# Where attention's masked sums are written, and where its row statistics are taken

## The chip, the cores and the metric

The kernel runs on one core of a Trainium2 chip. A core has a matrix engine (TensorE, PE in the profile, with its weight loads as PEld), VectorE (DVE), ScalarE (ACT), GpSimd (POOL) and SyncE (SP), whose queue issues most DMA transfers here. Each engine works through its own instructions in order and waits on semaphores for the others. The metric is device time in microseconds (us), the median over runs; lower is better.

## The reference, cut to what matters

Four layers act on `x` (2048 rows, width 512, fp32): a linear-attention layer A, a segmented attention layer B, and the same two again. Each normalizes its input's rows and adds its output to `x`.

```python
def _layernorm(x, axis=-1, eps=1e-5):
    m = jnp.mean(x, axis=axis, keepdims=True)
    v = jnp.var(x, axis=axis, keepdims=True)
    return (x - m) / jnp.sqrt(v + eps)
...
# layer B: 32 heads of width 16, 4 segments of 512 rows
for s in range(N):
    logits = jnp.einsum("bhqd,bhkd->bhqk", qs, ks) * scale + mask
    p = _softmax(logits, axis=-1)
    a_dot = jnp.einsum("bhqk,bhkd->bhqd", p, vs)
    ...
    a_mem = num / den
    o = g * a_mem + (1.0 - g) * a_dot
...
x = x + _A_ref(_layernorm(x, axis=-1), A_wqkv, A_w_phi, A_wo)
x = x + _B_ref(_layernorm(x, axis=-1), B_wq, B_wk, B_wv, B_wo, B_beta)
x = x + _A_ref(...)
x = x + _B_ref(...)
```

Two things bear on the change: every row of layer B's input needs its mean and variance, and every softmax row needs the maximum of its masked logits.

## The kernel before, in words

**Layer A** (`LayerA`) has two passes. `pass1` normalizes the rows, projects them and sums the key features. `pass2` goes through 16 tiles of 128 rows: it multiplies query features with the sums, divides (`weigh`, line 494), transposes and splits the result into a high and a low part (`turn`, line 465, tiles `oh` and `ol`), and multiplies by the output weights in `out_proj` (line 484). The end of `out_proj` is the function `end` (line 488): VectorE adds the product in PSUM to the rows of `x` (in a tile `xr` or `ot`, loaded by `residual`), and SP stores the sum to DRAM as layer B's input.

**Layer B** (`LayerB`) works in 4 segments of 512 rows. Per segment it normalizes the rows, projects queries, keys and values, and attends in 8 half-chunks `m` of 4 heads, so 32 half-chunks a layer and 64 in the kernel. Its `norm` (line 958) runs `norm_T` (line 426): load four tiles of rows into `x`; per tile `moments` (line 379: `bn_stats` and `bn_aggr` on VectorE, into a small tile `st`); `guard` adds the epsilon; `root` and `refine` make the inverse root; ACT normalizes each tile; `columns` transposes it. Each yield of this generator is placed by hand (`n`, `ln`, `load` in the tables).

For a half-chunk, `stack` lays the operands out by DMA (`e<-ta`); `maxima` (line 1150) finds each softmax row's maximum; `put_maxima` (line 1183) transposes the maxima, negates them on ACT into a tile `mt`, and stores them by a DMA of the ACT queue as one more row of the query operand, so that the exponential in `attend` (line 1192) needs no further subtraction. `maxima` has five passes. In each, PE writes logits into two PSUM banks, `mx` and `my`, of which there is one buffer each; then `top` (line 1163) runs on VectorE once per piece: add the mask, take the maximum, and write the masked sums back over the logits. The instruction that hands out the maximum appears in the profile as a second one, `DVE_READ_ACCUMULATOR2_ANT` on `mxs`. Three of the five passes hold two pieces per bank (widths 128 and 384, or twice 256), two hold a single piece of 512. The masked sums themselves are never read. PE's next pass needs the banks, and so waits for the last readout of each.

The memory part of layer B divides by denominators. `close` and `read` call `invert` (line 1038), which puts its steps on a calendar: `compact` loads 16 x 512 or 8 x 512 denominators into a tile `dn` (`dn<-den` on SP), `flip` takes the reciprocal on VectorE, `put` stores it (`inv<-dn` on SP), `spread` and `load` bring it back in the layout needed. In a layer's last segment, chunks 2 and 3 call it from `read`, so that its `compact` falls on the step of another chunk's `put`.

**What sets the order.** All engines are wrapped (`Ordered`, line 153), so each engine's instructions stay in the order in which the Python program issues them. In layer B that order comes from hand-written tables (`FIRST`, `GAPS`, `LAST`, `FINAL`, lines 52 to 101) with five steps per half-chunk: each step names the projections, norm steps and maxima to issue beside attention's own work. The end of layer A's pass 2 is issued inside the first steps of layer B (`steps`, line 1346, argument `side`; slots -9 to 1), and the beginning of layer B, with the norm of its first segment, inside pass 2 (`opening`, line 1331). Semaphore waits are worked out from the tiles: an instruction that writes a tile region waits for earlier readers and writers of it, on its own engine too, and a tile with `bufs=1` waits for the last use of its predecessor.

Of the kernel before, what the change touches and what calls it, by code (L numbers as in the profile page):

```python
# [18 lines left out]
P = 128  # L19
NSEG = 4  # L20
NC = D // P
NT = T // P
# [5 lines left out]
OT = 3  # L28
TA = 8
OO = 5  # L30
MT = 2
PV = 1
G = 3
R = 5
# [73 lines left out]
def interleave_kernel(ctx, tc, x_in, a_wqkv, a_wphi, a_wo, b_wq, b_wk, b_wv, b_wo, b_beta,  # L108
# [19 lines left out]
    def T2(tag, bufs, dt=F32, shape=(P, 512)):  # L128
        return sp.tile(list(shape), dt, tag=tag, bufs=bufs, name=nm(tag))
# [10 lines left out]
    def wait(f):  # L140

        if put_off[0] is None:
            f()
        else:
            put_off[0].append(f)
# [54 lines left out]
    share = cp.tile([P, 8], F32, name="share")  # L200
    gated = cp.tile([P, NC, 4], F32, name="gated")
    ones = cp.tile([32, P], F32, name="ones")

    def constants():

# [173 lines left out]
    def moments(st, t, x):  # L379
        bs = T2("bs", 2, shape=(P, 6))  # L380
        dve.bn_stats(bs, x)
        dve.bn_aggr(st[:, t, 0:2], bs)
# [40 lines left out]
            return wtiles(spare)  # L423
        return [hp_.tile([P, NC, D], F32R, tag=tag, bufs=1, name=nm(tag)) for tag in ("hh", "hl")]

    def norm_T(xsrc, s, hT, spare=None, slow=False, off=False):

        st = T2("st", 2, shape=(P, 4, 8))
        xt = rows_of(xsrc, s)
        yield  # L430
        for t, x in enumerate(xt):
            moments(st, t, x)
            if t < 3:
                yield
        guard(st)
        yield
        root(st)
        if slow:
            yield
        refine(st, pool if off else dve)  # L440
        if slow:
            yield
        for t in range(4):
            normal(st, t, xt[t])
            if slow and t < 3:
                yield
        yield
        hT[:] = htiles(spare)
        for t in range(4):
            columns(hT, t, xt[t])  # L450
            yield
# [32 lines left out]
    def out_proj(x, xdst, i, o, w):  # L484
        po = PS("g", G)
        yield from mm3(po, lambda a, kc: o[a][:, kc * P : (kc + 1) * P], lambda b, kc: w[b][:, kc, :])

        def end():
            dve.tensor_tensor(out=x, in0=po, in1=x, op=ADD)
            sync.dma_start(out=xdst[i], in_=x)  # L490
        wait(end)
        yield

# [106 lines left out]
    class LayerA:  # L600
# [4 lines left out]
        def first(self, hT, vv, upcoming):  # L605

            xt = rows_of(self.xsrc, SEGS[0])
            wph = T2("U", 2)[:, 0 : NC * DH].rearrange("p (c f) -> p c f", c=NC)
            sync.dma_start(out=ident, in_=c_ident)
            sync.dma_start(out=bd, in_=c_bd)  # L610
            sync.dma_start(out=wph, in_=a_wphi.rearrange("(c h) d f -> (h d) c f", c=NC))
            kraw, vraw, qraw = [fetch(a_wqkv[:, i * D : (i + 1) * D]) for i in (1, 2, 0)]
            st = T2("st", 2, shape=(P, 4, 8))
            hT[:] = htiles()
            (vh, vl), (kh, kl), (qh, ql) = wv, wk, wq = [wtiles(tag) for tag in ("w8", "w8", "e8")]
            for key, w in (("awv", wv), ("awk", wk), ("awq", wq)):
                kept[key] = [dtile((P, NC, D), nm(key)) for _ in range(2)]
                owed.extend(zip(kept[key], w))

            def low(eng, w, kc, raw):  # L620
                eng.tensor_tensor(out=w[1][:, kc, :], in0=raw, in1=w[0][:, kc, :].bitcast(F32), op=SUB)

            for t in range(4):
                moments(st, t, xt[t])
            guard(st)
            root(st)
            refine(st, dve)
            for c in range(NC):
                pool.tensor_tensor(out=phibd[:, c], in0=wph[:, c, :].unsqueeze(1).broadcast_to([P, 8, DH]),
                                        in1=bd[:, 16:24].unsqueeze(2).broadcast_to([P, 8, DH]), op=MUL)  # L630
            kf, qf = [], []
            kfold, qfold = folded(kraw, kf), folded(qraw, qf)
            normal(st, 0, xt[0])
            for t in (1, 3):
                dve.tensor_scalar(xt[t], xt[t], st[:, t, 2:3], st[:, t, 3:4], op0=MUL, op1=ADD)
            next(kfold)
            next(kfold)
            normal(st, 2, xt[2])
            columns(hT, 0, xt[0])
            columns(hT, 1, xt[1])  # L640
            next(kfold)
            next(kfold)
            columns(hT, 2, xt[2])
            columns(hT, 3, xt[3])
            next(kfold)
            upc = upcoming(1)
            next(upc[1])
            for kc in range(NC):
                act.copy(vh[:, kc, :], vraw[kc])
                low(pool if kc % 2 else dve, wv, kc, vraw[kc])  # L650
            for kc in range(NC):
                act.copy(kh[:, kc, :], kf[kc])
                low(dve, wk, kc, kf[kc])
            vt = v_tile(hT, wv, vv, ("g", G))
            for t in range(4):
                for _ in range(4):
                    next(vt)
                if t == 1:
                    for _ in range(4):
                        next(qfold)  # L660
                for _ in range(NEXT[t]):
                    next(upc[1])
            next(qfold)
            for kc in range(NC):
                act.copy(qh[:, kc, :], qf[kc])
                low(dve, wq, kc, qf[kc])
            return wq, wk, wv, upc
# [271 lines left out]
    class LayerB:  # L939
# [17 lines left out]

        def norm(self, s):
            self.hT[s] = []
            return norm_T(self.xsrc, s, self.hT[s], slow=True, off=True)  # L960

        def values(self, s):

# [74 lines left out]
        def invert(self, s, c, k, parts):  # L1038


            lo, hi = 8 * parts[0], 8 * parts[-1] + 8
            n = (hi - lo) * 4
            tiles = {}

            def compact():
                d = tiles["d"] = T2("dn", 2, shape=(P, 64))
                sync.dma_start(out=d[:, 0:n], in_=self.den(s, c)[lo:hi].rearrange("h (x i) -> (h x) i", i=n))

            def flip():
                dve.reciprocal(tiles["d"][:, 0:n], tiles["d"][:, 0:n])  # L1050

            def put():
                tiles["i"] = dtile((hi - lo, D), nm("inv"))
                sync.dma_start(out=tiles["i"].rearrange("h (x i) -> (h x) i", i=n), in_=tiles["d"][:, 0:n])

            def spread():
                wide = tiles["w"] = dtile((hi - lo, DH, D), nm("wide"))
                sync.dma_start(out=wide, in_=tiles["i"].unsqueeze(1).broadcast_to([hi - lo, DH, D]))

            def load():  # L1060
                for i in parts:
                    t = self.inv[s, c, i] = T2(*(("mmq", 2) if i else ("KN", 1)))
                    sync.dma_start(out=t, in_=tiles["w"][8 * i - lo : 8 * i - lo + 8].rearrange("h d n -> (h d) n"))
            for j, f in zip((0, 1, 2, 3, 5) if s < NSEG - 1 else (0, 2, 3, 4, 6), (compact, flip, put, spread, load)):
                self.at(k + j, f)
# [84 lines left out]
        def maxima(self, m):  # L1150


            s, c, hf = m // 8, m % 8 // 2, m % 2
            Q, K = [t[:, 2 * hf : 2 * hf + 2, :] for t in self.st[s, c]["set"]]
            mx = T2("mxs", 2, shape=(P, 16))

            def prod(pb, r, i, at, w):
                for e in range(2):
                    q, k = Q[64 * e : 64 * e + 63, r, :], K[64 * e : 64 * e + 63, r, :]
                    mm(pb[e][:, at : at + w], lhsT=q[:, i * P : (i + 1) * P], rhs=k[:, 0:w],  # L1160
                       start=True, stop=True, tile_position=(64 * e, 0))

            def top(pb, e, r, i, at):
                n = (i + 1) * P
                col = (e * 2 + r) * 4 + i
                pl = pb[e][:, at : at + n]
                with tc.high_priority():
                    dve.tensor_tensor_reduce(
                        out=pl, in0=pl, in1=mask[:, 512 - n : 512], scale=1.0, scalar=-3.0e38,
                        op0=ADD, op1=MAX, accum_out=mx[:, col : col + 1])  # L1170

            for what in ([(0, 0, 0), (0, 2, P)], [(0, 3, 0)], [(1, 0, 0), (1, 2, P)],
                         [(0, 1, 0), (1, 1, 256)], [(1, 3, 0)]):
                pb = [PS(t, 1) for t in ("mx", "my")]
                for r, i, at in what:
                    prod(pb, r, i, at, max(256, (i + 1) * P))
                for e in range(2):
                    for r, i, at in what:
                        top(pb, e, r, i, at)
                self.mx[m] = mx  # L1180
                yield

# [359 lines left out]
```

## Time and profile before

| | |
|---|---|
| median of 3 runs | 1481.35 us (1480.6 to 1843.29) |
| the profiled execution's own time | 1477.25 us |
| its span | 1475.5 us |
| granted TensorE clock, mean | 0.985 |
| stage: layer A 1, pass 1 | about 0 to 180 us |
| stage: pass 2, then its overlap with attention | about 180 to 270, and to 310 us |
| stage: attention 1 (layer B) | about 270 to 735 us |
| stage: layer A 2 | about 735 to 985 us, pass 1 to about 900 |
| stage: attention 2 | about 985 to 1475 us |

How to read it: the profile gives busy time of each engine and the idle time before its instructions with the engine and tile that ended it, in square brackets or behind `<-`. In a row such as `x512 | 254.8, 498 | 181.7 <-PE`, the numbers are the count, busy time in us, the mean of one in ns, and idle time before them. `mx<-mx,mask` means that tile `mx` is written from `mx` and `mask`. All operations recorded by a helper share that helper's line: L163 is the wrapper, L185 and L189 are the matmul helpers, so the tiles tell the operations apart. A VectorE row named `CUSTOM_DVE_ANT_0` is a `top`; `BATCH_NORM_STATS2` and `BATCH_NORM_AGGREGATE` are `moments`.

### The profile page before, as it was taken

The numbers are of one execution on the slowest core, as the hardware profiler recorded it, in microseconds if no ns is written. First come the engines' busy times: TensorE is split into PE (matmuls) and PEld (weight loads), VectorE is DVE, ScalarE is ACT, GpSimd is POOL, SyncE is SP. The second block draws the span as 40 slices with busy tenths as digits, with TensorE's granted clock in tenths as the row PEclk, the third lists the DMA queues.
The fourth block names the chain that finished last, engine by engine and source line by source line (L and its number), as shares of the span: only waits on it lengthen the run. The fifth ranks groups of instructions, "written<-read, shape, count | busy, mean of one in ns | idle before, by whom it ended". The sixth has DMA issues, their size and how long they took to land.

```text
span 1475.5 us, 32962 instructions
## 1 busy us (share of the span) xinstructions
PE 1395.7 (95%) x12052; PEld 960.0 (65%) x12052; DVE 1022.0 (69%) x3007; ACT 810.8 (55%) x1228; POOL 731.6 (50%) x1066
## 2 busy tenths in 40 slices
PE   7989999999999999998899999999999999999987
PEld 6778778765566566655567887886555565566544
DVE  4766877777667767677446677867776776766762
ACT  5546345446576576565534434543656766755652
POOL 1668754224455556454424456631345556645532
PEclk9999999999999999999999999999999999999998
DMA  5387375546556556567630105764565574565451
GB/s 189 115 293 245 114 245 166 164 133 176 155 145 202 167 147 200 161 182 195 205 129 32 50 30 183 220 184 116 152 178 140 148 235 141 153 203 162 121 187 44
DMA packets 139792, 236.33 MB, mean 160 GB/s; under 512 B 26576, under 2 KB 40016, under 8 KB 138864
## 3 DMA queue, kind: packets, MB, share of 16 engines
q1 hardware_dynamic: 138480, 233.70, 52.9%
q8 instruction: 97, 1.59, 0.5%
q10 hardware_dynamic: 1152, 0.52, 0.1%
q14 instruction: 63, 0.52, 0.1%
HBM read 129.17 MB, written 55.18 MB: 125 GB/s over the span
## 4 chain that ended last, share of the span: by engine, by line
PE 73%; DVE 10%; DMA 5%; ACT 5%; issue 3%; POOL 3%; SPq 1%; ACTq 0%; POOLq 0%; DVEq 0%
PE g L185 44%; PE pv L185 8%; PE lg L185 8%; PE mx L185 4%; PE g L189 4%; PE my L185 3%; DVE mx L163 2%; ACT P L163 2%; DMA dn<-den 2%; DVE my L163 2%; PE lg L189 1%; DVE es L163 1%; SPq L163 1%; POOL tmp L163 1%; POOL P L163 1%
## 5 line engine op out<-in xcount | busy, mean ns | idle before, releaser
L163 ACT ACTIVATE P<-lg 128x1024 f32<-128x1024 f32 x320 | 328.6, 1027 | 182.3 <-PE lg L185 168.9
L163 POOL TENSOR_SCALAR_AFFINE_SELECT P<-P 128x256 f32<-128x256 f32 (+1 forms) x448 | 190.2, 439 | 427.9 <-ACT P L163 421.6
L163 DVE CUSTOM_DVE_ANT_0 mx<-mx,mask 128x128 f32<-128x128 f32 (+3 forms) x512 | 254.8, 498 | 181.7 <-PE my L185 128.7
L163 DVE CUSTOM_DVE_ANT_0 my<-my,mask 128x128 f32<-128x128 f32 (+3 forms) x512 | 265.8, 519 | 6.5
L185 PE MATMUL lg<-e,e 64*128 64x256 f32 (+2 forms) x1024 | 170.5, 391 | 26.2 <-ACT P L163 26.1
L185 PE MATMUL g<-hh,wqk 128*128 128x512 f32 x512 | 185.0, 410 | 0.7 <-ACT mt L163 0.7
L185 PE MATMUL g<-w,oh 128*128 128x512 f32 x512 | 173.4, 420 | 2.4 <-ACT oh L163 2.4
L185 PE MATMUL pv<-P,v 128*32 128x512 f32 (+3 forms) x2048 | 168.4, 448 | 2.2 <-ACT ot L163 2.2
L185 PEld LDWEIGHTS lg<-e,e 64*128 64x128 f32 x1024 | 82.1, 186 | 126.5 <-issue 55.9
L185 PE MATMUL my<-e,e 63*128 63x256 f32 (+2 forms) x512 | 148.3, 350 | 12.5 <-DVE mxs L163 11.9
L185 PE MATMUL mx<-e,e 63*128 63x256 f32 (+2 forms) x512 | 146.6, 337 | 5.9 <-DVE mxs L163 5.8
L163 DVE DVE_READ_ACCUMULATOR2_ANT mxs<- 128x1 f32 x1024 | 145.1, 142 | 0.0
L185 PE MATMUL g<-w,hh 128*128 128x512 f32 x448 | 144.8, 404 | 0.0
L185 PEld LDWEIGHTS pv<-P,v 128*32 128x32 f32 x2048 | 54.5, 110 | 105.3 <-issue 92.4
L185 PEld LDWEIGHTS g<-hh,wqk 128*128 128x128 f32 x512 | 96.6, 189 | 31.6 <-issue 10.1
L185 PEld LDWEIGHTS g<-w,oh 128*128 128x128 f32 x512 | 90.7, 193 | 30.3 <-issue 11.0
L185 PEld LDWEIGHTS my<-e,e 63*128 63x128 f32 x512 | 84.6, 187 | 32.4 <-DVE mxs L163 11.2
L185 PE MATMUL g<-w,ol 128*128 128x512 f32 x256 | 103.9, 406 | 0.0
L185 PEld LDWEIGHTS mx<-e,e 63*128 63x128 f32 x512 | 90.7, 188 | 15.4 <-DVE mxs L163 5.1
L185 PE MATMUL g<-hl,wqk 128*128 128x512 f32 x256 | 100.6, 393 | 0.0
L185 PEld LDWEIGHTS g<-w,hh 128*128 128x128 f32 x448 | 81.6, 191 | 22.7 <-issue 6.1
L163 POOL TENSOR_TENSOR P<-P,es 128x512 f32<-128x512 f32 x32 | 49.0, 1531 | 85.9 <-DVE es L163 85.8
(156 smaller groups left out, 2682.7 us busy)
## 6 DMA issues: line engine op xcount, KB each, us to landing
e<-ta SPq DMA_DIRECT2D x384, 128.0 KB
wqk<-wqk SPq DMA_DIRECT2D x64, 512.0 KB
x<-x SPq DMA_DIRECT2D x48, 256.0 KB
wide<-inv SPq DMA_DIRECT2D x20, 512.0 KB
xr<-x SPq DMA_DIRECT2D x32, 256.0 KB
x<-xr SPq DMA_DIRECT2D x28, 256.0 KB
tmp<-U SPq DMA_DIRECT2D x56, 128.0 KB
KN<-wide SPq DMA_DIRECT2D x28, 256.0 KB
```

What stands on the lines that cost most here:

```text
L163: i = f(*a, **k)
L185: return held(nc.tensor.matmul(*a, **k))
L189: return held(nc.tensor.transpose(*a))
```

## The change

It has two parts, and room is made for them.

1. In passes with two pieces per bank, `top` writes its masked sums not over the logits but into `junk`, a tile of two slots of 384 one-byte elements in SBUF: the first piece of each bank into slot 0, the second into slot 1. The 512-wide pieces still write in place.
2. `end` in `out_proj` takes the mean and variance of the rows that it has just summed, into `stats`, a tile that holds 16 tiles' statistics. Layer B's `norm` hands its four tiles' slice of `stats` to `norm_T`, which then skips `moments` but keeps all its yields and still loads the rows.
3. `mt` and `dn` have one buffer instead of two; `st` is half as wide.

```diff
-MT = 2
+MT = 1
...
+    stats = cp.tile([P, NT, 4], F32, name="stats")
+    junk = cp.tile([P, 2, 384], mybir.dt.uint8, name="junk")
...
-    def norm_T(xsrc, s, hT, spare=None, slow=False, off=False):
+    def norm_T(xsrc, s, hT, spare=None, slow=False, off=False, st=None):
 
-        st = T2("st", 2, shape=(P, 4, 8))
+        known = st is not None
+        st = st if known else T2("st", 2, shape=(P, 4, 4))
         xt = rows_of(xsrc, s)
         yield
         for t, x in enumerate(xt):
-            moments(st, t, x)
+            if not known:
+                moments(st, t, x)
...
         def end():
             dve.tensor_tensor(out=x, in0=po, in1=x, op=ADD)
             sync.dma_start(out=xdst[i], in_=x)
+            moments(stats, i, x)
...
-            return norm_T(self.xsrc, s, self.hT[s], slow=True, off=True)
+            return norm_T(self.xsrc, s, self.hT[s], slow=True, off=True, st=stats[:, 4 * s : 4 * s + 4, :])
...
-                d = tiles["d"] = T2("dn", 2, shape=(P, 64))
+                d = tiles["d"] = T2("dn", 1, shape=(P, 64))
...
-            def top(pb, e, r, i, at):
+            def top(pb, e, r, i, at, spare):
...
-                        out=pl, in0=pl, in1=mask[:, 512 - n : 512], scale=1.0, scalar=-3.0e38,
+                        out=pl if spare is None else junk[:, spare, 0:n], in0=pl, in1=mask[:, 512 - n : 512], scale=1.0, scalar=-3.0e38,
...
-                    for r, i, at in what:
-                        top(pb, e, r, i, at)
+                    for j, (r, i, at) in enumerate(what):
+                        top(pb, e, r, i, at, j if len(what) > 1 else None)
```

More of the change, by code (lines that the diff above doesn't have):

```diff
@@ L612, in first @@
             kraw, vraw, qraw = [fetch(a_wqkv[:, i * D : (i + 1) * D]) for i in (1, 2, 0)]
-            st = T2("st", 2, shape=(P, 4, 8))
+            st = T2("st", 2, shape=(P, 4, 4))
             hT[:] = htiles()
```

## The prediction

> **What bounds the kernel now.** I read the page's busy line first, then TensorE's waits, then busy time by stage.
>
> ```profile
> PE 1395.7 (95%) x12052; PEld 960.0 (65%) x12052; DVE 1022.0 (69%) x3007; ACT 810.8 (55%) x1228; POOL 731.6 (50%) x1066
> ```
> ```profile
> PE lg L185 <- ACT P L163: 26.1, 31, 3.8
> PE my L185 <- DVE mxs L163: 11.9, 29, 0.6
> ...
> PE mx L185 <- DVE mxs L163: 5.8, 5, 2.4
> ```
> ```profile
> 180.00:270.00 90.00, 85.96 (x768) 71.12 (x766) 66.17 (x142) 45.44 (x76) 47.34 (x58) 0.98 0.64 200
> ...
> 530.00:660.00 130.00, 126.81 (x1016) 77.98 (x1014) 93.92 (x335) 84.88 (x123) 71.08 (x116) 1.00 0.60 171
> ```
>
> TensorE (PE) works for 1395.7 us of a span of 1475.5 us, and no matmul changes. Its idle time is 79.8 us; of that, waits for the maxima's readout (`mxs`, written by VectorE, DVE) are 11.9 + 5.8 = 17.7 us in 34 waits (columns: total, times, longest). A change on DVE alone can give back these and little else. In the windows (PE, PEld, DVE, ACT, POOL busy) DVE has about a quarter of each stage free, in pass 2 of the linear layer (180 to 270) as in attention (530 to 660).
>
> **The tops' output.** A pass over a pair of banks has two tops (masked sum and maximum) per bank in three passes out of five. The timeline of one such pass on DVE:
>
> ```profile
> 513.53 0.30 DVE L163 CUSTOM_DVE_ANT_0 mx<-mx,mask 128x128 f32<-128x128 f32 x1 [0.98 <-PE my L185]
> 513.75 0.14 DVE L163 DVE_READ_ACCUMULATOR2_ANT mxs<- 128x1 f32 x1
> 513.93 0.57 DVE L163 CUSTOM_DVE_ANT_0 mx<-mx,mask 128x384 f32<-128x384 f32 x1
> 514.41 0.14 DVE L163 DVE_READ_ACCUMULATOR2_ANT mxs<- 128x1 f32 x1
> 514.41 0.33 DVE L163 CUSTOM_DVE_ANT_0 my<-my,mask 128x128 f32<-128x128 f32 x1
> 514.66 0.14 DVE L163 DVE_READ_ACCUMULATOR2_ANT mxs<- 128x1 f32 x1
> 514.84 0.57 DVE L163 CUSTOM_DVE_ANT_0 my<-my,mask 128x384 f32<-128x384 f32 x1
> 515.32 0.14 DVE L163 DVE_READ_ACCUMULATOR2_ANT mxs<- 128x1 f32 x1
> 515.32 0.69 DVE L163 BATCH_NORM_STATS2 bs<-x 128x6 f32<-128x512 f32 x1
> ```
>
> In the program, the second top of a bank waits for the readout of the first, since both write that bank in place. It starts 513.93 - 513.75 = 0.18 us after the readout starts. A top without that wait (my at 514.41) starts with the readout ahead of it, and reaches its own readout after 0.25 us rather than 0.22. So a held second top costs 0.18 - 0.03 = 0.15 us. There are 3 passes x 2 banks x 64 half-chunks = 384 of them. With `junk` as the output, the wait that is left is for the top two places back (same slot of `junk`), whose readout ended earlier: my 128x128 at 514.41 would wait for the readout of 513.75, over by 513.89; my 128x384, at 514.66 at the soonest, for that of 514.41, over by 514.55. I take all 384 as freed: 384 x 0.15 = 58 us of DVE's time, 0.30 us per pass at the second bank. DVE's busy time falls less, since 0.03 of each 0.18 was idle already: 0.11 x 384 = 42 us, to about 980.
>
> Each top now writes one-byte elements to SBUF. No row has that. The nearest by operands (PSUM and SBUF in, SBUF out) is the residual's sum:
>
> ```profile
> L163 DVE CUSTOM_DVE_ANT_0 mx<-mx,mask 128x512 f32<-128x512 f32 x128 | 89.2, 697 | 74.1 <-PE my L185 61.2 <-PE mx L185 11.9
> ...
> L163 DVE BATCH_NORM_STATS2 bs<-x 128x6 f32<-128x512 f32 x64 | 43.4, 679 | 4.2 <-DMA x<-in 4.2
> ...
> L163 DVE TENSOR_TENSOR xr<-g,xr 128x512 f32<-128x512 f32 x40 | 27.5, 687 | 8.5 <-PE g L185 5.7 <-DMA xr<-x 2.8
> ...
> L163 DVE BATCH_NORM_AGGREGATE st<-bs 128x2 f32<-128x6 f32 x64 | 11.6, 182 | 2.2
> ...
> L163 DVE TENSOR_TENSOR w<-P,w 128x512 fp32r<-128x512 f32 x2 | 2.2, 1102 | 0.2 <-ACT w L163 0.2
> ```
>
> 687 against 697 ns: I take the place written as free. The bounds are 10 ns less per 512 elements, and the slowest row of the size, 1102 (405 ns more); the latter is a rival below.
>
> What of the 58 us lies on the path? Only where PE waits for `mxs`. First, smallest and last of attention 1's 15 waits at `my`, the bank that gets the whole 0.30:
>
> ```profile
> 280.41 0.35 PE L185 MATMUL my<-e,e 63*128 63x256 f32 x1 [0.56 <-DVE mxs L163]
> ...
> 361.19 0.47 PE L185 MATMUL my<-e,e 63*128 63x512 f32 x1 [0.22 <-DVE mxs L163]
> ...
> 691.51 0.38 PE L185 MATMUL my<-e,e 63*128 63x256 f32 x1 [0.27 <-DVE mxs L163]
> ```
>
> Thirteen of the 15 follow a two-top pass and shrink by 0.30 or to nothing: 11 x 0.30 + 0.25 + 0.22 = 3.8 us; two (the last among them) follow a single 512-wide top and keep their wait. At the same rate the 29 give 7.3 us. The five at `mx` (0.15 each, two of them caused elsewhere) give 0.5. Gain: 7.8 us. It could be less, to 4, if PE then stands longer at the 31 waits for ACT's exponential; I leave it whole, since ACT's input comes earlier with PE.
>
> A rule speaks against this. The Trainium skill, VectorE: DVE Perf Modes, section "The DRAIN you can't avoid", says that a semaphore after each of eight copies cost nothing over one after the last (13.88 us both ways), and advises counting operations, not semaphores. By it the gain would be nothing. The rows above differ: 0.18 against 0.00 from readout to next top.
>
> **The moved statistics.** 32 pairs of bn_stats and bn_aggr leave attention's norm and stand behind the residual's sum in the linear layer's `end`; DVE's total is unchanged, and so is the order on PE, ACT, POOL and SP. The store is issued ahead of them and waits for the sum alone. The buffer of x comes free one pair later; I name the store's own landing as the cover (2.8 us even for the smaller transfer quoted below). Behind the pair on DVE stands the next `ol` or top.
>
> ```profile
> 217.73 0.69 DVE L163 TENSOR_TENSOR xr<-g,xr 128x512 f32<-128x512 f32 x1 [0.63 <-PE g L185]
> 218.79 0.69 DVE L163 TENSOR_TENSOR ol<-pv,oh 128x512 fp32r<-128x512 f32 x1 [0.36 <-ACT oh L163]
> ...
> 260.57 0.68 DVE L163 BATCH_NORM_STATS2 bs<-x 128x6 f32<-128x512 f32 x1
> 261.29 0.18 DVE L163 BATCH_NORM_AGGREGATE st<-bs 128x2 f32<-128x6 f32 x1
> 261.39 0.66 DVE L163 BATCH_NORM_STATS2 bs<-x 128x6 f32<-128x512 f32 x1
> ```
>
> A pair takes 261.39 - 260.57 = 0.82 us. An iteration of pass 2 has gaps of 0.36 + 0.63 = 0.99 us on DVE, so a pair fits and costs nothing there. Where pass 2 overlaps the first maxima (272 to 292) DVE has no gaps: three pairs (2.46 us) against four two-top passes (1.2 us) leave it up to 1.2 us later. PE's wait at 280.41 and the next ones take some of that; without cover it is 1.2 a layer, with full cover 0. I take 0.7, 1.4 for both layers. The attention stages lose 12 pairs a layer, 12 x 0.82 = 9.8 us of DVE, mostly behind tops and off the path: I take 0, bound 1 us of gain. No wait for x's reload goes, since no attention row has one.
>
> **One buffer for `dn`, `mt`.** In the last segment a new `dn<-den` is issued right behind the `inv<-dn` of the other, on SP:
>
> ```profile
> 683.55 0.81 SPq L163 DMA_DIRECT2D inv<-dn  x1
> 684.40 0.43 SPq L163 DMA_DIRECT2D dn<-den  x1
> ...
> 689.81 0.35 DVE L163 RECIPROCAL dn<-dn 128x32 f32<-128x32 f32 x1 [2.82 <-DMA dn<-den]
> 690.86 0.38 PE L185 MATMUL mx<-e,e 63*128 63x256 f32 x1 [2.21 <-DVE mxs L163]
> ```
> ```profile
> 1397.32 0.39 SPq L163 DMA_DIRECT2D dn<-den  x1
> ...
> 1403.32 0.35 DVE L163 RECIPROCAL dn<-dn 128x32 f32<-128x32 f32 x1
> ```
> ```profile
> 1420.37 0.33 SPq L163 DMA_DIRECT2D dn<-den  x1
> 1423.20 0.55 DVE L163 RECIPROCAL dn<-dn 128x64 f32<-128x64 f32 x1 [0.47 <-DMA dn<-den]
> ```
>
> With one buffer SP waits there until `inv<-dn` has landed, at four places (two per layer); stores, residual loads and the operand pieces `e<-ta` queue behind. Landing took 2.83 us (1420.37 to 1423.20) and 5.41 us (684.40 to 689.81, with weight loads ahead). At 683.55 the store should land about 5.4 us on, near 689, and the read 2.8 us behind that, 691.8: the reciprocal, tops behind it and PE are 2 us later. At 1397.32 two landings of 2.8 us end at 1403.0, ahead of 1403.32: hidden. The other two read ahead as far and I take them as hidden. Cost: 2.0 us, from 0 to 4 x 5.4 = 21.6.
>
> `mt` now waits on ACT for its own last store:
>
> ```profile
> 322.09 0.50 ACTq L163 DMA_DIRECT2D e<-mt  x1
> ...
> 333.32 0.25 ACT L163 ACTIVATE mt<-g 16x128 fp32r<-16x128 f32 x1
> ```
>
> 11.2 us lie between, the closest of attention 1's first twenty; the slowest landing above is 5.4. Cost 0; without that cover the exponentials behind it on ACT would wait.
>
> **Sum.** -7.8 + 1.4 + 2.0 = -4.4 us. The profiled execution took 1477.25 us (1.75 around its span), so 1472.9 for such an execution. The median of the runs shown, 1481.35, is 4.1 above it; from there, 1477.0.
>
> **Rivals.**
> - Slower by the `dn` wait: one mechanism, SP standing at four places. It decides once more than 7.8 - 1.4 = 6.4 us of it reach PE. For it: at 690.86 PE already stands for this read. Against: the read of 1397.32 has 6 us. With two places exposed at 5.4: -6.4 + 10.8 = +4.4, 1485.8; all four: 1496.6.
> - The tops gain nothing, because the waits two back or the extra wait instructions hold DVE as before: +1.4 + 2.0, 1484.8. The Trainium skill's rule above would give this too.
> - One-byte output is slow, as the 1102 ns row: 405 ns x 256/512 (mean width) = 0.2 us on each of 768 tops, four per pass, 0.8 - 0.3 = 0.5 us more on each of 34 waits: 17 + 3.4, 1502; new waits could pass 2%.
> - More gain: all 17.7 us of the waits go and the costs hide: 1463.7.
>
> **How the numbers follow.** Forecast 0.62 (1470 to 1483), `dn` 0.13, no gain 0.10, slow output 0.07, more gain 0.08. The range 1466 to 1490 holds the forecast, no gain, and the part of `dn` with up to two places, 0.08: 0.80. Some 2% is what a measurement here tells from no change, 1451.7 to 1511.0: faster 0.01; slower 0.025 (from slow output with new waits, and a little of `dn`); same 0.965.
>
> **What would show it.** Second tops that start with the readout ahead of them; DVE busy near 980; PE's `my` waits near 4.6 us; bn_stats, still 64, half of them on xr and ot; SP idle between `inv<-dn` and `dn<-den` in the last segments, and the wait of 2.82 at 689.81 near 4.8. Wrong it would be if the second tops still start 0.18 late, if 128x384 tops take longer than 0.57 us, or if PE's waits for ACT grow by what the `mxs` waits lose.

## The result, and the profile after

The changed kernel takes 1464.76 us (median of 4 runs, 1459.9 to 1469.2) against 1481.96 us: a ratio of 0.9886, 95% interval [0.9845, 0.9928]. The forecast of a small gain had the right sign, but 17 us were gained where 4.4 were forecast, and the time lies just below the range (1466). One run of the kernel before took 1843.29 us, far from its other three, and is left out of the ratio. The other runs of one kernel spread by over 1%, and the longer ones tend to have the lower granted TensorE clock: before's slowest and fastest of 20 in a later comparison are 1488.46 us at a clock of 0.980 and 1468.69 us at 0.989. So one profile against another says where time went, and the ratios of many runs say how much.

The page of the changed kernel, and TensorE's (PE's) waits (total us, times, longest):

```profile
PE 1377.6 (94%) x12052; PEld 950.1 (65%) x12052; DVE 953.2 (65%) x3007; ACT 809.1 (55%) x1228; POOL 731.5 (50%) x1066
```
```profile
PE lg L185 <- ACT P L163: 30.8, 38, 3.8
PE mx L185 <- DVE mxs L163: 11.0, 7, 4.4
...
PE my L185 <- DVE mxs L163: 3.4, 15, 0.3
...
PE g L185 <- DVE ol L163: 1.6, 5, 0.5
```

The span is 1461.6 us, 13.9 less. VectorE (DVE) is busy 68.8 us less. But PE's idle time has not fallen: 1461.6 - 1377.6 = 84.0 us against 79.8. The waits for the maxima's readout went from 17.7 to 14.4 us only. The waits for ACT's exponential (`lg`) rose from 26.1 to 30.8. What shrank is PE's *busy* time, by 18.1 us, with not one matmul changed. A part of that may be the clock, 0.990 in this profile and 0.985 before; but in E1 below, with the tops changed alone, the clock is 0.986 and PE is busy 1378.9 us, 16.8 less. This is the puzzle that the prediction's step did not allow for.

A two-top pass on DVE now:

```profile
509.74 0.29 DVE L163 CUSTOM_DVE_ANT_0 junk<-mx,mask 128x128 uint8<-128x128 f32 x1 [0.97 <-PE my L185]
509.95 0.08 DVE L163 DVE_READ_ACCUMULATOR2_ANT mxs<- 128x1 f32 x1
509.95 0.55 DVE L163 CUSTOM_DVE_ANT_0 junk<-mx,mask 128x384 uint8<-128x384 f32 x1
510.43 0.08 DVE L163 DVE_READ_ACCUMULATOR2_ANT mxs<- 128x1 f32 x1
510.43 0.28 DVE L163 CUSTOM_DVE_ANT_0 junk<-my,mask 128x128 uint8<-128x128 f32 x1
510.64 0.08 DVE L163 DVE_READ_ACCUMULATOR2_ANT mxs<- 128x1 f32 x1
510.64 0.55 DVE L163 CUSTOM_DVE_ANT_0 junk<-my,mask 128x384 uint8<-128x384 f32 x1
511.12 0.08 DVE L163 DVE_READ_ACCUMULATOR2_ANT mxs<- 128x1 f32 x1
511.12 0.17 DVE L163 TENSOR_SCALAR stats<-stats 128x4 f32<-128x4 f32 x1
```

Every second top starts with the readout ahead of it, as forecast, and readouts are shorter too (0.08 us for 0.14). The pass takes 511.12 - 509.74 = 1.38 us instead of 515.32 - 513.53 = 1.79.

Where PE's busy time went shows in the matmuls of one pass over the banks. First a pass of the kernel before in which both banks were free, then one in which `my` was late, both with the matmul that follows; last the same pass as the second one, in the changed kernel:

```profile
302.84 0.39 PE L185 MATMUL mx<-e,e 63*128 63x512 f32 x1
302.84 0.39 PE L185 MATMUL my<-e,e 63*128 63x512 f32 x1
303.16 0.73 PE L185 MATMUL g<-w,oh 128*128 128x512 f32 x2
...
360.57 0.40 PE L185 MATMUL mx<-e,e 63*128 63x512 f32 x1
361.19 0.47 PE L185 MATMUL my<-e,e 63*128 63x512 f32 x1 [0.22 <-DVE mxs L163]
361.59 1.28 PE L185 MATMUL pv<-P,v 128*32 128x384 f32 x16
```
```profile
355.15 0.40 PE L185 MATMUL mx<-e,e 63*128 63x512 f32 x1
355.28 0.47 PE L185 MATMUL my<-e,e 63*128 63x512 f32 x1
355.68 1.28 PE L185 MATMUL pv<-P,v 128*32 128x384 f32 x16
```

The program places the matmuls into `mx` and `my` at different rows of the array (`tile_position` 0 and 64), and where both banks are free they start together (302.84): from there to the start of the next work is 0.32 us. With `my` 0.62 us late it is 361.59 - 360.57 = 1.02 us, and of that delay the profile calls only 0.22 us idle; during the rest `mx` runs alone, and PE counts as busy. In the changed kernel the lag is 0.13 us and the pass takes 0.53. Pairing each matmul into `my` with that into `mx`, by their starts in the traces (512 pairs), `my` lags `mx` by 49.6 us in total before and by 33.1 after. Before, 133 pairs lie over 0.1 us apart; the rows of idle time at `my` list 29 waits.

### The profile page after: what moved, and what is told of

Same layout as the page of the kernel before. It is cut to its first block, busy times and chain, and to the rows that moved or that the text cites. A ratio compares the mean times of both kernels' runs of the same rounds, so it can differ in the third digit from the quotient of the medians.

```text
span 1461.6 us, 33122 instructions
## 1 busy us (share of the span) xinstructions
PE 1377.6 (94%) x12052; PEld 950.1 (65%) x12052; DVE 953.2 (65%) x3007; ACT 809.1 (55%) x1228; POOL 731.5 (50%) x1066
## 4 chain that ended last, share of the span: by engine, by line
PE 72%; DVE 8%; ACT 7%; DMA 6%; issue 3%; POOL 3%; SPq 1%; ACTq 0%; POOLq 0%; DVEq 0%
PE g L185 45%; PE pv L185 7%; PE lg L185 7%; PE mx L185 4%; PE g L189 4%; ACT P L163 3%; PE my L185 3%; PE lg L189 2%; POOL tmp L163 1%; DMA inv<-dn 1%; DVE junk L163 1%; DMA e<-ta 1%; DMA dn<-den 1%; DVE es L163 1%; ACT tb L163 1%
## 5 line engine op out<-in xcount | busy, mean ns | idle before, releaser
L163 DVE CUSTOM_DVE_ANT_0 junk<-mx,mask 128x128 uint8<-128x128 f32 (+2 forms) x384 | 146.7, 420 | 129.6 <-PE my L185 95.8
L185 PE MATMUL lg<-e,e 64*128 64x256 f32 (+2 forms) x1024 | 169.2, 388 | 31.0 <-ACT P L163 30.8
L163 DVE CUSTOM_DVE_ANT_0 mx<-mx,mask 128x512 f32<-128x512 f32 x128 | 89.1, 696 | 108.0 <-PE my L185 92.6
L163 DVE CUSTOM_DVE_ANT_0 junk<-my,mask 128x128 uint8<-128x128 f32 (+2 forms) x384 | 146.7, 419 | 0.1
L185 PEld LDWEIGHTS g<-hh,wqk 128*128 128x128 f32 x512 | 96.9, 189 | 32.3 <-issue 10.9
L163 DVE DVE_READ_ACCUMULATOR2_ANT mxs<- 128x1 f32 x1024 | 100.0, 98 | 0.0
```

The source lines that it names most:

```text
L163: i = f(*a, **k)
L185: return held(nc.tensor.matmul(*a, **k))
```

## The experiments

Times are medians; each ratio is of the runs to the runs of the kernel before on the same chip. E1 to E4 share their runs of before (1480.91 us), E5 to E8 theirs (1478.42); E9's is 1483.41.

**E1, the tops alone.** Statistics stay in attention's norm.

```diff
 (the changed kernel)
-    stats = cp.tile([P, NT, 4], F32, name="stats")
...
-            moments(stats, i, x)
...
-            return norm_T(self.xsrc, s, self.hT[s], slow=True, off=True, st=stats[:, 4 * s : 4 * s + 4, :])
+            return norm_T(self.xsrc, s, self.hT[s], slow=True, off=True)
```

> The changed kernel with the statistics left in attention's norm; the masked sums go to the small tile, mt and dn have one buffer. Theory 'tops': the faster tops carry the whole gain, so this run stands at 0.986 to 0.992 of the kernel before (1461 to 1470 us), DVE busy near 953. Rival 'statistics': the moved pairs free DVE in attention and carry about half, so 0.993 to 0.997 here. Rival 'no cause in the change' (run to run drift): 0.998 to 1.002.

1462.26 us, 0.9877 [0.9839, 0.9914]; lag of `my` 29.3 us, DVE busy 953.6. The tops carry the whole gain, within what the intervals can tell.

**E2, the statistics alone.** All tops write in place.

```diff
 (the changed kernel)
-    junk = cp.tile([P, 2, 384], mybir.dt.uint8, name="junk")
...
-                        out=pl if spare is None else junk[:, spare, 0:n], in0=pl, in1=mask[:, 512 - n : 512], scale=1.0, scalar=-3.0e38,
+                        out=pl, in0=pl, in1=mask[:, 512 - n : 512], scale=1.0, scalar=-3.0e38,
```

> The changed kernel with all masked sums written in place as before; statistics moved, mt and dn with one buffer. Theory 'tops': no gain, and the price of the dn wait (2 us) and of pairs in the crowded stretch (1.4 us): 1.000 to 1.004. Rival 'statistics': 0.993 to 0.997. Rival 'no cause in the change': 0.998 to 1.002, as in the run of the tops.

1479.45 us, 0.9999 [0.9972, 1.0026]; lag 53.8 us. No gain. The interval holds "nothing" as well as the lower part of the small cost that was forecast. The theory that freed VectorE time in attention carries half falls.

**E3, two buffers for `dn`.**

```diff
 (the changed kernel)
-                d = tiles["d"] = T2("dn", 1, shape=(P, 64))
+                d = tiles["d"] = T2("dn", 2, shape=(P, 64))
```

> The changed kernel with two buffers for dn again. If the wait of SP for the store of dn costs what the first layer's last segment shows, the reciprocal near 687 us waits about 2.5 us less and the time is 2 to 3 us below the changed kernel (about 1462, ratio 0.9865 to before). If the wait is hidden, the same time as the changed kernel.

1464.64 us, 0.9895 [0.9853, 0.9938]: no difference from the changed kernel that these runs can tell; but the interval holds the 0.9865 of the first forecast too, so the time decides nothing. The place itself, in the changed kernel and then in E3 (SP's issues, the reciprocal, PE):

```profile
679.94 0.53 SPq L163 DMA_DIRECT2D inv<-dn  x1
685.37 0.32 SPq L163 DMA_DIRECT2D dn<-den  x1
...
687.10 0.35 DVE L163 RECIPROCAL dn<-dn 128x32 f32<-128x32 f32 x1 [4.96 <-DMA dn<-den]
...
688.15 0.58 PE L185 MATMUL mx<-e,e 63*128 63x256 f32 x1 [4.43 <-DVE mxs L163]
```
```profile
683.43 0.53 SPq L163 DMA_DIRECT2D inv<-dn  x1
684.01 0.42 SPq L163 DMA_DIRECT2D dn<-den  x1
...
688.18 0.35 DVE L163 RECIPROCAL dn<-dn 128x32 f32<-128x32 f32 x1 [4.06 <-DMA dn<-den]
...
689.24 0.58 PE L185 MATMUL mx<-e,e 63*128 63x256 f32 x1 [3.53 <-DVE mxs L163]
```

With one buffer SP stands 5.4 us between the two issues, with two 0.6 us; the reciprocal's wait differs by 0.9 us only. The load issued at 684.01 ended that wait 4.2 us later, the one issued at 685.37 only 1.7 us later. The two profiles do not meet the place alike, since in E3 SP came to `inv<-dn` 3.5 us later. But the kernel before and E2, both with tops in place, give about the same difference: 2.82 us with two buffers (the prediction's line), 3.89 with one.

**E4, tops in turns.** In place, but mx, my, mx, my: the wait is for the top two back, and nothing else changes.

```diff
 (the kernel before)
-                for e in range(2):
-                    for r, i, at in what:
+                for r, i, at in what:
+                    for e in range(2):
                         top(pb, e, r, i, at)
```

> The kernel before with the tops of a pass in another order: first piece of mx, first of my, second of mx, second of my. All write in place, but none waits for the readout just ahead of it. If the held wait alone makes tops dear, second tops start with the readout ahead of them and the 384 waits' 0.15 us go: DVE busy near 980, time 0.990 to 0.996. If the place written sets the length of the readout and of the top, readouts stay at 0.14 us and DVE gains only part. As mx is released one top later, the gain could also vanish on PE's path: 0.998 to 1.002.

1467.91 us, 0.9914 [0.9886, 0.9942]; DVE busy 983.8, lag 32.1 us. Its DVE timeline:

```profile
512.54 0.30 DVE L163 CUSTOM_DVE_ANT_0 mx<-mx,mask 128x128 f32<-128x128 f32 x1 [1.16 <-PE my L185]
...
513.01 0.60 DVE L163 CUSTOM_DVE_ANT_0 mx<-mx,mask 128x384 f32<-128x384 f32 x1
513.52 0.14 DVE L163 DVE_READ_ACCUMULATOR2_ANT mxs<- 128x1 f32 x1
513.52 0.60 DVE L163 CUSTOM_DVE_ANT_0 my<-my,mask 128x384 f32<-128x384 f32 x1
514.04 0.14 DVE L163 DVE_READ_ACCUMULATOR2_ANT mxs<- 128x1 f32 x1
514.04 0.69 DVE L163 BATCH_NORM_STATS2 bs<-x 128x6 f32<-128x512 f32 x1
```

The pass takes 1.50 us, 0.29 less: just the held waits. Readouts in place stay at 0.14 us. So of the changed kernel's 0.41 us per pass, 0.29 is the wait and 0.12 goes with the new output, and by the medians the wait alone gives most of the time (the intervals of E4 and E1 overlap).

**E5, the mirror.** The kernel before, with `my`'s tops ahead of `mx`'s. PE still issues `mx` first, so it now stands idle where it used to run `mx` alone.

```diff
 (the kernel before)
-                for e in range(2):
+                for e in (1, 0):
                     for r, i, at in what:
                         top(pb, e, r, i, at)
```

> The kernel before with the banks' tops in the other order: both of my first, then both of mx; TensorE still issues mx's matmuls first. Theory 'overlap': matmuls into mx and my run at the same time when both banks are free, so a late my costs its whole delay even where mx runs alone meanwhile and no idle time shows. Then holding mx as well changes nothing: 0.997 to 1.003, while the idle time before mx put down to the readout grows from 5.8 to 30 us or more and TensorE's busy time falls by about as much. Rival, the prediction's own step: only idle rows cost time, so the added idle time adds to the span, 1.015 to 1.025.

1481.2 us, 1.0013 [0.9984, 1.0043]; the lag is 2.8 us.

```profile
PE mx L185 <- DVE mxs L163: 30.6, 50, 3.1
```

The same pass in the kernel before and here, with the matmul ahead of it:

```profile
278.87 0.60 PE L189 MATMUL pv<-ident,tmp 128*128 128x128 f32 x4
279.50 0.35 PE L185 MATMUL mx<-e,e 63*128 63x256 f32 x1
280.41 0.35 PE L185 MATMUL my<-e,e 63*128 63x256 f32 x1 [0.56 <-DVE mxs L163]
280.42 0.38 PE L185 MATMUL mx<-e,e 63*128 63x256 f32 x1
280.60 0.28 PE L185 MATMUL my<-e,e 63*128 63x256 f32 x1
```
```profile
278.47 0.60 PE L189 MATMUL pv<-ident,tmp 128*128 128x128 f32 x4
280.01 0.35 PE L185 MATMUL mx<-e,e 63*128 63x256 f32 x1 [0.94 <-DVE mxs L163]
280.01 0.38 PE L185 MATMUL my<-e,e 63*128 63x256 f32 x1
280.20 0.28 PE L185 MATMUL mx<-e,e 63*128 63x256 f32 x1
280.24 0.28 PE L185 MATMUL my<-e,e 63*128 63x256 f32 x1
```

From the start of the matmul ahead to that of the last one of the pass it is 1.73 us before and 1.77 here; the idle rows say 0.56 and 0.94. Over the whole kernel, idle time at `mx` went from 5.8 to 30.6 us while the 11.9 us at `my` vanished, 12.9 us more in all, at no cost that the runs show: the interval ends at 6 us. So most of that delay was in the kernel before all along, inside PE's busy time. An estimate over all passes agrees: counted from the start of the matmul ahead to that of the pass's last one, above the quickest twentieth of the passes behind such a matmul, the passes lose about 53 us before, 58 in E5 and 39 in E1. PE's busy time fell by 8.7 us (1395.7 to 1387.0, both at a clock of 0.985), not by the 25 that were expected: that number had left out the waits at `my` that go, and this execution is 6.1 us longer. The rival, that idle rows are all the cost, asked for 1.5% or more; with the waits at `my` taken off it asks for 0.9%, still outside the interval, and falls. A small cost is not excluded: at a clock of 0.985 the two runs of E5 took 1483.34 and 1484.74 us, the three of before on that chip 1477.08 to 1478.9.

**E6, all tops.** The 512-wide tops write to the small tile as well, now two slots of 512.

```diff
 (the kernel of E1)
-    junk = cp.tile([P, 2, 384], mybir.dt.uint8, name="junk")
+    junk = cp.tile([P, 2, 512], mybir.dt.uint8, name="junk")
...
-                        top(pb, e, r, i, at, j if len(what) > 1 else None)
+                        top(pb, e, r, i, at, j if len(what) > 1 else e)
```

> As the run with the tops alone, and the 512-wide tops go to the small tile too (one slot of 512 per bank). If the shorter readout holds for them (0.08 for 0.14 us), my is free about 0.1 us earlier after 128 more passes; by the theory of overlap that takes 2 to 4 us off the run with the tops alone, 0.985 to 0.987. If only the held second tops mattered, no change: 0.988.

1458.19 us, 0.9862 [0.9825, 0.99]; lag 24.9 us against 29.3 in E1; all readouts now take 83 ns on average, against 98 in E1, where a quarter of the tops still write in place. As forecast by the theory of overlap, but the interval holds E1's ratio.

**E7, two-byte elements.**

```diff
 (the kernel of E1)
-    junk = cp.tile([P, 2, 384], mybir.dt.uint8, name="junk")
+    junk = cp.tile([P, 2, 384], BF16, name="junk")
```

> As the run with the tops alone, with two-byte (bf16) elements in the small tile. If the place (SBUF for PSUM) makes readouts and tops shorter, readouts stay at 0.08 us and the time at 0.988. If the one-byte element does, readouts and tops are nearer to those in place (0.14 us) and the time nearer to the run in turns, 0.991.

1462.52 us, 0.9884 [0.9847, 0.9921]. One row of E7, one of the changed kernel, and one of E4:

```profile
L163 DVE CUSTOM_DVE_ANT_0 junk<-mx,mask 128x384 bf16<-128x384 f32 x128 | 70.7, 553 | 0.0
```
```profile
L163 DVE CUSTOM_DVE_ANT_0 junk<-mx,mask 128x384 uint8<-128x384 f32 x128 | 70.7, 553 | 0.0
```
```profile
L163 DVE CUSTOM_DVE_ANT_0 mx<-mx,mask 128x384 f32<-128x384 f32 x128 | 76.5, 598 | 0.0
```

553 ns for one byte and for two, 598 in place: the one-byte element is not what makes the top shorter. Whether the place does it or the width of four bytes is not shown, since no run wrote four-byte masked sums to SBUF.

**E8, the reciprocal later.** The changed kernel's largest waits at `mx` (3.3, 4.4 and 2.6 us) stand right behind a reciprocal that is ahead of the tops on DVE and waits for its load (687.10 and 688.15 in the lines under E3). It moves to the step of its store.

```diff
 (the kernel of E1)
-            for j, f in zip((0, 1, 2, 3, 5) if s < NSEG - 1 else (0, 2, 3, 4, 6), (compact, flip, put, spread, load)):
+            for j, f in zip((0, 2, 2, 3, 5) if s < NSEG - 1 else (0, 3, 3, 4, 6), (compact, flip, put, spread, load)):
```

> As the run with the tops alone, with the reciprocal of dn one step later, at the step of its store. Theory 'dn next': TensorE's six waits at mx (10.6 us) stem from this reciprocal standing on VectorE ahead of the tops, waiting for its load; one step later (about 2.7 us) they shrink, 5 to 8 us less, 0.982 to 0.985. Rival: the queue of SP is late there anyway (ACT waits for the same stretch's weight loads), TensorE stands elsewhere: 0.988.

1457.43 us, 0.9843 [0.98, 0.9886], 5 us below E1. Waits at `mx` for the readout, 10.6 us in E1, are 0.9 us in two waits; DVE's waits for the load fell from 21.9 to 10.9 us. The point estimate agrees with 'dn next'; the intervals of E1 and E8 overlap.

**E9, both.** E6 and E8 in one kernel.

> All tops to the small tile (two slots of 512) and the reciprocal of dn one step later; statistics left in attention's norm. If the two gains have different causes (my's lag after single passes; the reciprocal ahead of the tops), they add: 0.9862 and 0.9843 against 0.9877 for the tops alone give 0.981 to 0.984. If both meet the same next wait (ACT's exponential), no better than the later reciprocal alone: 0.984 to 0.986.

1450.82 us, 0.9779 [0.9741, 0.9818]: the fastest here, and its interval lies below the changed kernel's. That is beyond the forecast of 0.981 to 0.984 by its median, and the interval excludes the rival (0.984 to 0.986). So the two together do better than the later reciprocal alone was to do; but as the intervals of E6 and E8 hold E1's ratio or meet its interval, and E8's meets that of E9, these runs do not show how much each adds. PE's waits in E9:

```profile
PE lg L185 <- ACT P L163: 35.1, 39, 3.8
...
PE my L185 <- DVE mxs L163: 2.8, 13, 0.2
```

The largest wait left is that for ACT's exponential, 26.1 us before; whether a faster exponential would give time was not tried.

## Why the prediction was wrong

**The held second top: right.** The 0.15 us per held top and the 384 tops came out: 0.29 us per pass in E4 where 0.30 was forecast, and DVE busy 983.8 where 980 was. What the Trainium skill (VectorE: DVE Perf Modes, "The DRAIN you can't avoid") measured on eight copies, that a semaphore after each costs nothing extra, does not carry over to these tops: E4 adds and removes no operation, only moves who waits for whom, and gains 0.9%. (The advice to count operations, not semaphores, stands in the same page of the Trainium skill under "Rules for kernel authors".)

**The place written: a small miss.** It was taken as free, by the residual's row (687 against 697 ns). The new output gives 0.12 us more per pass: readouts of 0.08 for 0.14 us, and shorter tops where they overlap a readout (553 against 598 ns). DVE's busy time, forecast near 980 us, is 953.2. The rival of a slow one-byte output falls with E7's and the changed kernel's rows.

**The share on the path: this step failed.** The prediction said of the 17.7 us of idle rows: "A change on DVE alone can give back these and little else", and made the gain 7.8 us from 34 waits. The tops alone gave 0.9877, about 18 us. The rows of idle time before a matmul hold only the part of a late bank in which PE runs nothing. While `mx` runs without its partner, PE counts as busy, and that cost as much: at 361.19 the row says 0.22 us where the pass lost 0.70 (1.02 against 0.32). The lag of `my`, 49.6 us, was the larger sum to read; the tops alone took 20.3 us off it. E5 supports that such lag is paid: its pass takes as long with the lag turned into idle time. The table adds the lag to the waits at `mx` for the readout, from one profile of each run, and sets the change of that sum beside the change of the median time (us):

| run | lag of `my` | waits at `mx` | sum, against before | time, against before |
|---|---|---|---|---|
| before | 49.6 | 5.8 | | |
| E2, statistics alone | 53.8 | 10.6 | +9.0 | -1.5 |
| changed kernel | 33.1 | 11.0 | -11.3 | -17.2 |
| E4, in turns | 32.1 | 10.3 | -13.0 | -13.0 |
| E7, two-byte elements | 29.3 | 11.4 | -14.7 | -15.9 |
| E3, two buffers for `dn` | 31.1 | 9.4 | -14.9 | -16.3 |
| E1, tops alone | 29.3 | 10.6 | -15.5 | -18.7 |
| E6, all tops | 24.9 | 11.1 | -19.4 | -20.2 |
| E8, reciprocal later | 30.9 | 0.9 | -23.6 | -21.0 |
| E9, both | 24.2 | 0.7 | -30.5 | -32.6 |

The time follows the sum in the runs that are faster. E2 does not fit, and the sum leaves out what else moved, the waits for ACT's exponential above all, which rose by 4 to 9 us in the faster runs. E5 is not in the table, since its delay stands in idle rows, and these begin only where the profile lets the matmul ahead end. So the table supports the account and is not a full one.

The prediction's own sign of being wrong came up as well: the waits for ACT's exponential grew by 4.7 us while those for `mxs` fell by 3.3. By idle rows there was nothing to gain, and yet 17 us were gained. And the rival "more gain" named 1463.7 us, close to the 1464.76 measured, but by luck: it let all 17.7 us of the waits go, and 14.4 are still there.

**The moved statistics: size near, place not.** 1.4 us was forecast for pairs in the crowded stretch (272 to 292 us). PE's waits for `ol` appear where the statistics are moved (1.6 us in five waits, above) and not in E1 or before. But they lie at 196, 305, 911, 1020 and 1438 us, none in that stretch, and the last is not theirs, since E4 has one there too. The four others make 1.4 us; that the size agrees is luck. DVE's own wait ahead of `ol` for ACT falls from 13.4 us to 5.3, as was forecast for the gaps that the pairs fill. E1 and E2 bound their whole effect within noise of nothing.

**One buffer for `dn`: right in place, half in size.** The wait at that reciprocal was to go from 2.82 to near 4.8 us, and is 4.96. But E3 shows 4.06 with two buffers, and E4, whose tops are faster too, 4.01: over half of the growth comes with the faster tops, which reach the load earlier. The buffer's own share is 0.9 us (changed kernel against E3) or 1.1 (E2 against before), not 2.0, and no time shows for it. DVE's waits for loads of `dn` rose from 16.7 to 23.6 us in all; what the tops gained was in part given back there, and E8 took the waits at `mx` behind them away. `mt` cost little: PE's waits for it are 0.7 and 0.2 us before and after, and ACT's one new row, a wait of `P` for the store of `mt` (2.0 us, once), stands in the changed kernel and E1 but not in E2 or E3; E5, with two buffers, has such a row as well (1.3 us), so it does not tell of the buffer.

**What stays open.** Some of the difference between single runs goes with the granted clock (0.990 in the changed kernel's profile, 0.985 before). Whether the change itself raises it, through a steadier use of TensorE, was not tried; at the same clock of 0.985 single runs still stand at 1469.2 us (changed), 1463.07 (E1) and 1477.08 to 1481.08 (before, six runs on two chips). Why E2 is no slower than before, with more lag and longer waits at `mx` in its profile, is open too.

## What to carry to other kernels

Where two matmuls run at the same time, compare their starts: here a late partner cost its delay, and of 49.6 us of it the profile listed 11.9 as idle. A chain of operations on one engine that write the same bank in turn can pay for each wait on its direct predecessor, here 0.15 us; interleave two banks, or send an output that nobody reads elsewhere. When one engine gets faster, look for the load that its next instruction waits for: here those waits grew from 16.7 to 23.6 us, and what stood behind them gave a part of the gain back.

## What the runs showed of the hardware

The readout of a maximum takes 0.14 us behind a top that writes fp32 sums in place in PSUM (142 ns on average in E4) and 0.08 behind one that writes elements of one byte (83 ns in E6) or of two (E7) to SBUF. A top of 128x384 that starts with a readout ahead of it takes 598 ns in the first case and 553 in the second.

A second top that waits for the readout just ahead of it starts 0.18 us after that readout starts; one that waits for the readout two back, or for none, starts with the readout ahead of it (E4, changed kernel).

Matmuls at `tile_position` 0 and 64 start together when both banks are free (302.84 before).

The load of `dn` ended its reader's wait 5.4 us after its issue when it was issued 1.9 us behind the issue of eight weight loads (before, 684.40), 4.2 us when 2.6 us behind (E3), and 1.7 us when 6.8 us behind (changed kernel). That fits a small load which stands behind larger ones, but no run moved them, so it is not shown.
